# Reordering the hand-over and the close of a fused attention, soft-MoE and ELU feed-forward kernel

## The chip, the cores and the metric

The kernel runs on one core of a Trainium2 chip. The metric is the device time of one execution in microseconds; less is better. Before the change three runs took 362.8, 362.89 and 364.88 us, with a median of 362.89 us. A core has a matrix engine (TensorE, PE in the profile; its weight loads are PEld), VectorE (DVE), ScalarE (ACT), GpSimd (POOL) and SyncE (SP), which here only issues transfers. Each engine works through its own instructions strictly in order and waits on semaphores for the others. Matrix products land in PSUM, from which VectorE and ScalarE copy them to SBUF.

## What is computed

```python
for t in range(S):                                  # B=4, H=8, S=768, D=48
    state = alpha[:, :, t, :, None] * state + k_t v_t^T
    y[:, :, t] = q_t state
x = y as (3072, 384)
logits = x @ phi                                    # 32 slots
d = softmax of logits over tokens;  c = softmax of logits over slots
slot_out[e] = relu(slot_input[e] @ w1[e]) @ w2[e]   # 8 experts, slot_input = d.T @ x
x = c @ slot_out
h = x @ w_in                                        # 384 -> 2048
out = elu(h) @ w_out                                # 2048 -> 384
```

The inputs are float64 words for `w_in` and `w_out`, which the kernel converts itself, and float32 for the rest.

## The kernel before

**Stages.** Up to about 182 us the attention recurrence runs in 24 units of 128 tokens. Then come the slot softmax and, from about 202 to 231 us, the eight experts. The stage around the change follows: the expert result `o_ps` is scaled by `den` into `so`, turned (`st_ps`, `sot`) and multiplied with `w_in` into G (`g_ps`, 32 slots by 2048, laid out as four row groups of 32 by 512 columns and made in two halves x = 0, 1 of 256 columns). G is split into a rounded part `ghi` and the rest `glo`, and `g_part(x)` spreads each half into `gst` by small products (`selr`) into the banks `r_ps`, three of which are the banks `z_ps` of the last stage.

**The last stage** is a loop of 48 pairs p (6 groups of 512 tokens, 16 blocks of 128 hidden columns each, two blocks to a pair). Step 2p runs `ffn_h(p)` (two products `hf_ps`) and `ffn2(p - 2)` (six products into `z_ps`); step 2p + 1 runs `ffn_m(p)` (ScalarE makes `mm`, the ReLU of minus h, in a ring of three) and `ffn_r(p)` (r: VectorE squares the pair's first block, GpSimd its second). `hf_ps` has two buffers, so `ffn_h(p + 2)` can only start when r(p) has been read. ELU is not evaluated exactly on this path: the hidden values are small, so the kernel uses h plus half of min(h, 0) squared; the linear part is the product `gw` of G with `w_out`, added to each group's result.

**Converting w_out.** Sixteen pieces m of `w_out` are converted on the fly: `cvo_hi(m)` is two VectorE instructions (`f64_hi`, lines 85 and 87), `round_wo(m)` one of ScalarE (line 872), both needed by `ffn2(m // 2)`; `cvo_lo(m)` is one of ScalarE, one of VectorE (`f64_lo`, lines 93 and 94) and one of GpSimd (line 710), needed only by `gw_part`.

**What sets the order.** It is written out by hand. `at_place(k)` is called behind every expert and every step (place 15 + i stands behind step i) and runs whatever the tables name for that place: `HI`, `RD` and `LO` for the three conversions of each m, `GTW` for turning G, the four `gw_part` and `gw_end`, `CLOSE` for the 12 late additions, `CHK` for the checks. The late additions belong to groups 0 to 3, whose results are stored aside before gw is known: `close(i)` makes one product `cg_ps` in the single buffer `ps_f` and VectorE adds it. Groups 4 and 5 take gw as a third product in `z_ps` (line 1016).

**The end.** The checks leave one number `bad`. Behind the last step every engine loads it into a register (line 1074) and branches (line 1075) over `general_path`, a slow exact path that the inputs here never take, to the end of the program.

Of the kernel before, what the change touches and what calls it, by code (L numbers as in the profile page):

```python
# [10 lines left out]
F32 = mybir.dt.float32  # L11
# [59 lines left out]
HI = [9, 9, 9, 9, 10, 11, 12, 13, 14, 15, 16, 18, 20, 22, 24, 26]  # L71
RD = [9, 9, 11, 11, 12, 14, 15, 16, 17, 19, 20, 22, 24, 26, 28, 30]
LO = [15 + 14 + 10 * m // 3 for m in range(16)]

GTW = [35, 55, 57, 81, 83, 85]
CHK = [44, 54, 82, 94]
NLATE = 4
CLOSE = [87 + 3 * i // 2 for i in range(3 * NLATE)]
# [19 lines left out]
def general_path(tc, ctx, qka, vt, phi, w1, w2, w_in, w_out, out):  # L98
# [16 lines left out]
    for b in range(B):  # L115
        for j in range(NP):
# [36 lines left out]
    for u in range(NU):  # L153
# [4 lines left out]
        A_.copy(xt, xt_ps)  # L158
# [32 lines left out]
    for u in range(NU):  # L191
        t_ps = gp.tile([NS, 128], F32, tag="t", name="g_cps")
        T.matmul(out=t_ps, lhsT=cc[:, u, :], rhs=ident, start=True, stop=True)
        A_.copy(ct[:, 128 * u:128 * u + 128], t_ps)
# [3 lines left out]
    for d in range(ND):  # L198
# [4 lines left out]
        A_.copy(si[:, d, :], s_ps)  # L203
    so = gk.tile([128, ND, NS], F32, name="g_so")
    for e in range(NE):
# [6 lines left out]
        for f in range(8):  # L212
# [4 lines left out]
            A_.activation(ht[:, f, :], h_ps, AF.Relu)  # L217
        for d in range(ND):
# [4 lines left out]
            A_.copy(so[:, d, own], o_ps)  # L223

    def f64(src, dst):
# [6 lines left out]
        f64_lo(nc, w[:, :, 0], aa, dst, pp)  # L232
# [5 lines left out]
    for n in range(4):  # L238
# [5 lines left out]
        A_.copy(gs[:, 512 * n:512 * n + 512], acc[0][0:NS])  # L244
# [6 lines left out]
    for t in range(NG):  # L251
        cols = slice(TG * t, TG * t + TG)
        for f in range(NFT):
            h_ps = gp.tile([128, TG], F32, tag="h", name="g_fps")
            T.matmul(out=h_ps, lhsT=gs[:, 128 * f:128 * f + 128], rhs=ct[:, cols], start=True, stop=True)
            n_ = gw.tile([128, TG], F32, tag="n", name="g_n")
            V.tensor_scalar_min(n_, h_ps, 0.0)
            ex = gw.tile([128, TG], F32, tag="e", name="g_e")
# [3 lines left out]
            V.scalar_tensor_tensor(out=ex, in0=h_ps, scalar=0.0, in1=ex, op0=ALU.max, op1=ALU.add)  # L262
            for d in range(ND):
                T.matmul(out=acc[d], lhsT=wo[:, f, 128 * d:128 * d + 128], rhs=ex, start=(f == 0), stop=(f == NFT - 1))
        z = gw.tile([128, ND, TG], F32, tag="z", name="g_z")
        for d in range(ND):
            A_.copy(z[:, d, :], acc[d])
# [855 lines left out]
```

## Time and profile before

| | |
|---|---|
| Median of three runs | 362.89 us |
| Profiled execution | 366.09 us, of which its span 364.2 us |
| TensorE busy in the span | 296.0 us (81%) |
| VectorE busy | 271.6 us (75%) |
| ScalarE busy | 206.3 us (57%) |
| GpSimd busy | 176.6 us (49%) |
| Chain that ended last | VectorE 45%, TensorE 39% |
| Mean granted TensorE clock | 0.916 |

In the profile, times are microseconds from the span's start. The granted clock has two levels here: 1.00 is 2.4 GHz, 0.50 is 1.2 GHz. A float32 product is two matmul instructions, so "x6" is the six instructions of one pair's products into `z_ps` in the loop (their operands are rounded to one instruction each). Line numbers are those of the kernel before; behind line 80 the changed kernel's numbers are up to 15 higher.

### The profile page before, as it was taken

Reading aid. Unit: us, or ns where it says so; the run is one execution under the profiler, and the core shown is the slowest. Engines: PE = TensorE matmul, PEld = TensorE weight load, DVE = VectorE, ACT = ScalarE, POOL = GpSimd, SP = SyncE. Lnnn points to the kernel's source line nnn. Section 1 sums busy time; section 2 is a strip of 40 time slices with the busy share of each in tenths; the row PEclk is TensorE's granted clock in tenths of the full one; section 3 lists DMA queues with packets and bytes.
Section 4 is the critical chain, followed back from the end, with each engine's and each line's share of the span. In section 5 each row is a group of like instructions: output and inputs, shape, how many; then the busy total and the mean of one; then the engine's idle time right before and its main releaser. Section 6 shows DMA issues by size and latency. Waiting matters only on the chain.

```text
span 364.2 us, 9069 instructions
## 1 busy us (share of the span) xinstructions
PE 296.0 (81%) x3594; PEld 214.6 (59%) x3594; DVE 271.6 (75%) x542; ACT 206.3 (57%) x432; POOL 176.6 (49%) x242
## 2 busy tenths in 40 slices
PE   8666876976968786687788999868999999998991
PEld 4655755754656565565565545336877577665781
DVE  5999999999999999999952342568876546654641
ACT  1556676766857676676675222365776566533340
POOL 4364665566545564554651021013687869733340
PEclk9998798799889889888969999866999999998998
DMA  7559769795995877877179899900000000004422
GB/s 287 168 154 279 267 203 290 224 301 165 288 284 181 261 233 244 277 243 237 53 254 354 339 418 416 385 7 0 0 2 1 0 0 3 0 3 173 161 99 95
DMA packets 22354, 66.88 MB, mean 184 GB/s; under 512 B 2464, under 2 KB 8608, under 8 KB 21408
## 3 DMA queue, kind: packets, MB, share of 16 engines
q1 hardware_dynamic: 22016, 64.65, 51.7%
q10 hardware_dynamic: 288, 1.58, 1.1%
q8 instruction: 30, 0.49, 0.6%
q14 instruction: 20, 0.16, 0.1%
HBM read 61.50 MB, written 4.72 MB: 182 GB/s over the span
## 4 chain that ended last, share of the span: by engine, by line
DVE 45%; PE 39%; issue 10%; ACT 2%; DMA 2%; ACTq 0%
PE z_ps L1012 17%; DVE sfx L416 8%; DVE r L443 6%; PE hf_ps L985 6%; DVE cva L87 5%; DVE cvb L85 4%; PE h_ps L840 3%; DVE sn L521 3%; PE z_ps L862 2%; DVE wi L654 2%; DVE ring L421 2%; DVE pr L429 2%; DMA ring<-qka 2%; DVE wo L87 2%; PE g_ps L913 1%
## 5 line engine op out<-in xcount | busy, mean ns | idle before, releaser
L1012 PE MATMUL z_ps<-rr,wor 128*128 128x512 f32 x288 | 77.7, 405 | 0.8 <-DVE gst L1063 0.8
L997 POOL TENSOR_TENSOR rr<-mm 128x512 fp32r<-128x512 f32 x48 | 50.2, 1052 | 56.4 <-ACT mm L990 55.6
L990 ACT ACTIVATE mm<-hf_ps 128x1024 f32<-128x1024 f32 x48 | 48.9, 1028 | 32.4 <-PE hf_ps L985 23.3
L1012 PEld LDWEIGHTS z_ps<-rr,wor 128*128 128x128 f32 x288 | 55.5, 194 | 15.3 <-DVE gst L1063 1.6
L551 PE MATMUL y_ps<-vsr,r 128*64 128x64 f32 x768 | 42.7, 250 | 24.7 <-ACT vsr L291 24.1
L551 PEld LDWEIGHTS y_ps<-vsr,r 128*64 128x64 f32 x768 | 34.0, 158 | 34.6 <-ACT vsr L291 29.7
L996 DVE SCALAR_TENSOR_TENSOR rr<-hf_ps,mm 128x512 fp32r<-128x512 f32 x48 | 33.0, 690 | 26.7 <-ACT mm L990 26.5
L531 POOL TENSOR_TENSOR sp<-sn,sfx 128x192 f32<-128x192 f32 x44 | 23.9, 542 | 56.2 <-DVE sn L521 41.0
L479 POOL TENSOR_SCALAR_AFFINE_SELECT r<-at 64x512 f32<-64x512 f32 x48 | 39.2, 817 | 13.1 <-ACT at L472 10.2
L291 ACT COPY vsr<-sp 48x192 f32<-48x192 f32 x88 | 30.7, 349 | 17.4 <-POOL sp L531 16.2
L466 PE MATMUL at_ps<-r,ring 64*64 64x64 f32 x768 | 36.6, 244 | 4.2 <-DVE r L443 2.1
L291 ACT COPY r<-r 64x512 f32<-64x512 f32 x24 | 14.8, 615 | 38.9 <-DVE r L443 38.9
L466 PEld LDWEIGHTS at_ps<-r,ring 64*64 64x64 f32 x768 | 31.8, 155 | 7.7 <-issue 4.0
L985 PE MATMUL hf_ps<-cst,gst 128*128 128x512 f32 x96 | 32.5, 421 | 3.7 <-DVE rr L996 3.1
L651 POOL TENSOR_TENSOR wi<-wi,cvb 128x256 f32<-128x256 f32 x24 | 28.2, 1173 | 12.0 <-ACT xt L291 4.3
L416 DVE TENSOR_TENSOR_SCAN sfx<-ring,imp 128x520 f32<-128x520 f32 x24 | 30.2, 1260 | 2.3 <-DMA ring<-qka 2.3
L429 DVE TENSOR_TENSOR_SCAN pr<-ring,ini 128x520 f32<-128x520 f32 x24 | 31.1, 1295 | 0.8
L985 PEld LDWEIGHTS hf_ps<-cst,gst 128*128 128x128 f32 x96 | 17.7, 195 | 11.8 <-DVE rr L996 3.7
L443 DVE TENSOR_TENSOR r<-ring,pr 128x512 f32<-128x512 f32 x24 | 24.2, 1007 | 0.0
L710 POOL TENSOR_TENSOR wo<-wo,pp 128x384 bf16<-128x384 f32 x16 | 17.2, 1077 | 7.4 <-DVE pp L94 4.1
L454 PE MATMUL kt_ps<-ident,ring 128*128 128x128 f32 x96 | 17.8, 315 | 2.9 <-DVE ring L421 2.9
L508 PE MATMUL kv_ps<-vpr,kt 64*48 64x48 f32 x352 | 19.4, 219 | 0.0
(175 smaller groups left out, 542.5 us busy)
## 6 DMA issues: line engine op xcount, KB each, us to landing
ring<-qka SPq DMA_DIRECT2D x22, 772.5 KB, 5.4
w<-w SPq DMA_DIRECT2D x24, 512.0 KB, 5.1
w<-w SPq DMA_DIRECT2D x7, 1536.0 KB, 9.1
raw<-w_in SPq DMA_DIRECT2D x24, 256.0 KB, 2.8
wo<-w_out SPq DMA_DIRECT2D x8, 768.0 KB, 15.0
vsr<-vs SPq DMA_DIRECT2D x48, 96.0 KB, 4.9
out<-wi SPq DMA_DIRECT2D x4, 768.0 KB, 3.8
ring<-qka ACTq DMA_DIRECT2D x2, 772.5 KB, 7.6
```

The source lines that it names most:

```text
L291: (e.copy if e is A_ else e.tensor_copy)(out, in_)
L416: V.tensor_tensor_scan(out=flat(sfx)[:, ::-1], data0=a[:, 1:ACOL + 1][:, ::-1], data1=flat(imp)[:, ::-1], initial=0.0, op0=ALU.mult, op1=A ...
L429: V.tensor_tensor_scan(out=flat(pr), data0=a[:, 0:ACOL], data1=flat(ini), initial=0.0, op0=ALU.mult, op1=ALU.add)
L443: eng["q"][0].tensor_mul(split(r[:, 0]), split(qs(u)), st[u].pop("pr")[:, :, 1:])
L466: T.matmul(out=at_ps[64 - p0:128 - p0, j, t0:t0 + C], lhsT=k[p0:p0 + 64, j, t0:t0 + C], rhs=r[p0:p0 + 64, h2, j, t0:t0 + C], start=True, s ...
L479: G.affine_select(out=split(r[p0:p0 + 64, h2]), in_=split(at[p0:p0 + 64]), pattern=[[0, 2 * NP], [1, C]], compare_op=ALU.is_ge, fill=0.0, ...
L551: T.matmul(out=y_ps[t0:t0 + C, 2 * j + h2, :], lhsT=r[:, h2, j, t0:t0 + C], rhs=vsr[u % RING][:, h2, g, D * j:D * j + YW], start=True, sto ...
L985: T.matmul(out=h_ps[:, x, :], lhsT=gst[:, 128 * f:128 * f + 128], rhs=cst[:, TG * grp:TG * grp + TG], start=True, stop=True)
L990: A_.activation(m, hp[p], AF.Relu, scale=-1.0)
L996: V.scalar_tensor_tensor(out=r[0], in0=h[:, 0], scalar=-1.0, in1=m[:, 0], op0=ALU.mult, op1=ALU.mult)
L997: G.tensor_mul(r[1], m[:, 1], m[:, 1])
L1012: T.matmul(out=z_ps[j], lhsT=wo[:, cols], rhs=rs[x], start=(i == 0), stop=(late and i == NFT - 1))
```

## The change

Five things, all behind the experts. (1) `g_ps` becomes two PSUM tiles, one for each half of G; `so` is made by ScalarE alone; one small product (`busy2(1)`) stands behind `sot`, and six products into a tile `idle` behind `ffn_h(1)`. (2) The tables of conversions: of the three `cvo_hi` between the second half of G and r(0), one moves ahead of that half and one behind r(0), the `cvo_lo` are spread from place 25 to 73 (before: 29 to 79). (3) `mm` has four places instead of three. (4) The four `gw_part` stand together at place 76, `gw_end` at 77, the checks at 44, 54, 60 and 70, and the 12 late additions at 81, 83, ..., 103, one for each pair (before: two in each run of three places from 87 on). (5) In the last group ScalarE evacuates all three banks, SP stores the first and ScalarE the other two in one transfer; the register load moves up to ahead of step 92; the general path's ScalarE copies go to VectorE, so that ScalarE has about a quarter of the instructions to branch over.

```diff
-HI = [9, 9, 9, 9, 10, 11, 12, 13, 14, 15, 16, 18, 20, 22, 24, 26]
+HI = [9, 9, 9, 9, 10, 10, 11, 12, 14, 17, 18, 20, 22, 24, 26, 28]
-LO = [15 + 14 + 10 * m // 3 for m in range(16)]
+LO = [15 + 10 + 16 * m // 5 for m in range(16)]
-GTW = [35, 55, 57, 81, 83, 85]
-CHK = [44, 54, 82, 94]
+GTW = [35, 76, 76, 76, 76, 77]
+CHK = [44, 54, 60, 70]
-CLOSE = [87 + 3 * i // 2 for i in range(3 * NLATE)]
+CLOSE = [81 + 2 * i for i in range(3 * NLATE)]
...
-    A_.activation(so[:, 0:256], o_ps[:, 0:256], AF.Copy, scale=den)
-    V.tensor_scalar_mul(so[:, 256:], o_ps[:, 256:], den)
+    A_.activation(so, o_ps, AF.Copy, scale=den)
...
     A_.copy(sot, st_ps)
+    busy2(1)
...
-    g_t = ps_h.tile([128, 2, 512], F32, tag="h", name="g_ps")
-    g_ps = [g_t[:, x, 0:256] for x in range(2)]
+    g_ps = [ps_h.tile([128, 2, 512], F32, tag="h", name="g_ps")[:, 0, 0:256] for x in range(2)]
...
-        mp[p] = m = mm[:, 2 * TG * (p % 3):2 * TG * (p % 3 + 1)].rearrange("p (x t) -> p x t", x=2)
+        t, x = (mm, p % 4) if p % 4 < 3 else (end, 2)
+        mp[p] = m = t[:, 2 * TG * x:2 * TG * (x + 1)].rearrange("p (x t) -> p x t", x=2)
...
-                (A_.copy if j == 1 else V.tensor_copy)(z[:, j, :], z_ps[j])
-                if grp == NG - 1:
-                    SY.dma_start(out=out[:, j, toks], in_=z[:, j, :])
+                last = grp == NG - 1
+                (A_.copy if last or j == 1 else V.tensor_copy)(z[:, j, :], z_ps[j])
+                if last and j == 0:
+                    SY.dma_start(out=out[:, 0, toks], in_=z[:, 0, :])
+                elif last and j == ND - 1:
+                    A_.dma_start(out=out[:, 1:, toks], in_=z[:, 1:, :])
...
     for i in range(2, NK + 4):
+        if i == NK - 4:
+            b = nc.values_load(bad[0:1, 0:1], min_val=0, max_val=1,
+                               skip_runtime_bounds_check_because="a comparison gave it")
         ffn_step(i)
+        if i == 2:
+            idle = ps_f.tile([128, 128], F32, tag="f", name="idle")
+            for _ in range(6):
+                T.matmul(out=idle, lhsT=ident, rhs=ident, start=True, stop=True)
```

The diff of `general_path` (ScalarE's copies become VectorE's, two ELU blocks share an activation), of `f64_lo` (which takes the multiplying engine as an argument) and of `RD` (two entries one place earlier or later) is left out.

VectorE between the first subtraction into `glo` (line 917, now 921) and the second r: two instructions of lines 85 and 87 are one `cvo_hi`, 1063 (1071) are the copies of `g_part`, 996 (1001) is r. Before:

```order
L85 TENSOR_SCALAR pp<-wo_3178 128x384
L87 SCALAR_TENSOR_TENSOR wo_3178<-wo_3178,pp 128x384
L1063 CAST gst<-z_ps_3019 128x256
L1063 CAST gst<-z_ps_3021 128x256
L85 TENSOR_SCALAR pp<-wo_3189 128x384
L87 SCALAR_TENSOR_TENSOR wo_3189<-wo_3189,pp 128x384
L85 TENSOR_SCALAR pp<-wo_3189 128x384
L87 SCALAR_TENSOR_TENSOR wo_3189<-wo_3189,pp 128x384
L996 SCALAR_TENSOR_TENSOR rr_3440<-hf_ps,mm 128x512
```

Now, at the same place:

```order
L921 TENSOR_TENSOR gst<-g_ps,gst 128x256
L1071 CAST gst<-z_ps_3019 128x256
L1071 CAST gst<-z_ps_3021 128x256
L85 TENSOR_SCALAR pp<-wo_3189 128x384
L87 SCALAR_TENSOR_TENSOR wo_3189<-wo_3189,pp 128x384
L1001 SCALAR_TENSOR_TENSOR rr_3442<-hf_ps,mm 128x512
L1071 CAST gst<-z_ps_3019 128x256
L1071 CAST gst<-z_ps_3021 128x256
```

Between the second half's `glo` and r(0) one conversion stands instead of three, and none stands between r(0) and the second copies of `g_part`.

TensorE in the close: 974 (978) is the late addition's product, 1040 the product of the check, 985 `hf_ps`, 1012 one bank of `z_ps`. Before, at the places 93 and 94:

```order
L974 MATMUL cg_ps<-cst,gwst 128x512 x2
L1040 MATMUL n_ps<-ok_3444,ok_3443 1x1
L985 MATMUL hf_ps<-cst,gst 128x512 x2
L1012 MATMUL z_ps_3019<-rr_3440,wor_3493 128x512 x2
L1012 MATMUL z_ps_3020<-rr_3440,wor_3493 128x512 x2
```

Now, for every pair from place 81 on:

```order
L978 MATMUL cg_ps<-cst,gwst 128x512
L989 MATMUL hf_ps<-cst,gst 128x512 x2
L1017 MATMUL z_ps_3019<-rr_3442,wor_3369 128x512 x2
L1017 MATMUL z_ps_3020<-rr_3442,wor_3369 128x512 x2
L1017 MATMUL z_ps_3021<-rr_3442,wor_3369 128x512 x2
```

Two products that share the one buffer of `ps_f` no longer follow each other.

ScalarE's last rows: 990 (995) makes `mm`, 1017 (1023) evacuates a bank. Before:

```order
L990 ACTIVATE mm<-hf_ps 128x1024 x7
L1017 COPY zz<-z_ps_3020 128x512
L1074 TENSOR_LOAD bad
L1075 COMPARE_AND_BRANCH
```

Now:

```order
L1081 TENSOR_LOAD bad
L995 ACTIVATE mm<-hf_ps 128x1024
L995 ACTIVATE end<-hf_ps 128x1024
L1023 COPY zz<-z_ps_3019 128x512
L1023 COPY zz<-z_ps_3020 128x512
L1023 COPY zz<-z_ps_3021 128x512
L1027 DMA out<-zz 128x2x512
L1089 COMPARE_AND_BRANCH
```

VectorE's and SP's part of the last evacuation has moved to ScalarE, and the register load stands two pairs earlier, as on all engines.

## Rows read from the trace of the kernel before

**Rows 1.** The page: the span and the number of instructions.
```profile
span 364.2 us, 9069 instructions
```
**Rows 2.** Stretches: length, each engine's busy time, granted clock, DMA share, GB/s.
```profile
234.80:241.60 6.80, 5.46 (x52) 2.16 (x44) 1.95 (x5) 2.00 (x5) 0.00 (x0) 0.50 0.22 87
245.00:251.90 6.90, 4.48 (x10) 3.09 (x11) 6.80 (x12) 3.63 (x7) 2.59 (x3) 0.51 0.00 0
251.90:320.00 68.10, 66.87 (x313) 49.36 (x312) 43.90 (x75) 43.74 (x57) 49.55 (x48) 1.00 0.00 1
333.90:337.10 3.20, 3.20 (x9) 2.52 (x8) 0.69 (x1) 1.02 (x1) 1.04 (x1) 0.50 0.65 246
```
**Rows 3.** TensorE's waits, 230 to 252 us: total, times, longest.
```profile
PE hf_ps L985 <- DVE rr L996: 2.0, 1, 2.0
PE g_ps L913 <- ACT end L919: 1.3, 1, 1.3
PE z_ps L1012 <- DVE gst L1063: 0.8, 1, 0.8
...
PE st_ps L899 <- DVE end L894: 0.4, 1, 0.4
```
**Rows 4.** Instructions in time, 226 to 262 us: start, length, engine, what, [wait].
```profile
230.73 0.58 ACT L872 ACTIVATE wor<-wo 128x384 fp32r<-128x384 f32 x1 [2.27 <-DVE wo L87]
...
231.32 0.94 PE L791 MATMUL z_ps<-ident 128*128 128x128 f32 x6
...
244.49 1.42 DVE L87 SCALAR_TENSOR_TENSOR wo<-wo,pp 128x384 int32<-128x384 int32 x1
...
246.57 1.22 PE L985 MATMUL hf_ps<-cst,gst 128*128 128x512 f32 x2 [2.03 <-DVE rr L996]
...
248.64 2.92 PE L1012 MATMUL z_ps<-rr,wor 128*128 128x512 f32 x6 [0.85 <-DVE gst L1063]
```
**Rows 5.** The chain that ended last: start, length, what.
```profile
305.36 0.46 PE hf_ps L985 x2
305.82 1.38 PE z_ps L1012 x6
...
356.73 0.69 DVE zz L1017
```
**Rows 6.** Groups by line, VectorE, 252 to 320 us: busy, mean ns, idle before.
```profile
L996 DVE SCALAR_TENSOR_TENSOR rr<-hf_ps,mm 128x512 fp32r<-128x512 f32 x32 | 22.0, 692 | 20.3 <-ACT mm L990 20.2
...
L94 DVE TENSOR_SCALAR pp<-wo 128x384 int32<-128x384 int32 x16 | 10.9, 683 | 0.0
...
L87 DVE SCALAR_TENSOR_TENSOR wo<-wo,pp 128x384 int32<-128x384 int32 x4 | 2.2, 559 | 0.1
L85 DVE TENSOR_SCALAR pp<-wo 128x384 int32<-128x384 int32 x3 | 2.1, 694 | 0.0
```
**Rows 7.** TensorE's waits, 252 to 320 us.
```profile
PE hf_ps L985 <- DVE rr L996: 1.1, 2, 0.6
```
**Rows 8.** TensorE's waits, 320 to 358 us.
```profile
PE cg_ps L974 <- DVE wi L975: 2.3, 3, 0.8
PE n_ps L1040 <- DVE wi L975: 0.8, 1, 0.8
```
**Rows 9.** The branch over the general path: count, ns, first and last start.
```profile
L1075 SPq EVENT_SEMAPHORE  x8: 17/17/17, 362.3 to 362.8; - x8
...
L1075 ACTq COMPARE_BRANCH  x1: 50/50/50, 356.6 to 356.6; - x1
...
L1075 SPq COMPARE_BRANCH  x1: 45/45/45, 358.7 to 358.7; - x1
L1075 ACTq EVENT_SEMAPHORE  x1: 17/17/17, 359.2 to 359.2; - x1
```
**Rows 10.** The last stores: count, KB each, median us from issue to landing.
```profile
out<-zz SPq DMA_DIRECT2D x1, 768.0 KB, 3.8
out<-zz SPq DMA_DIRECT2D x3, 256.0 KB, 2.6
```

More of the change, by code (lines that the diff above doesn't have):

```diff
@@ L157, in general_path @@
         xt = gw.tile([128, ND, 128], F32, tag="xt", name="g_xt")
-        A_.copy(xt, xt_ps)
+        V.tensor_copy(xt, xt_ps)
         l_ps = gp.tile([NS, 128], F32, tag="t", name="g_lps")
@@ L167, in back @@
             T.transpose(t_ps, src[:, 128 * u:128 * u + 128], ident[0:NS, 0:NS])
-            A_.copy(dst[:, u, :], t_ps)
+            V.tensor_copy(dst[:, u, :], t_ps)
     cc = gk.tile([128, NU, NS], F32, name="g_cc")
@@ L193, in general_path @@
         T.matmul(out=t_ps, lhsT=cc[:, u, :], rhs=ident, start=True, stop=True)
[L194 removed]
+        V.tensor_copy(ct[:, 128 * u:128 * u + 128], t_ps)
     si = gk.tile([128, ND, NS], F32, name="g_si")
@@ L202, in general_path @@
                      stop=(u == NU - 1))
-        A_.copy(si[:, d, :], s_ps)
+        V.tensor_copy(si[:, d, :], s_ps)
     so = gk.tile([128, ND, NS], F32, name="g_so")
@@ L222, in general_path @@
                          stop=(f == 7))
-            A_.copy(so[:, d, own], o_ps)
+            V.tensor_copy(so[:, d, own], o_ps)
     def f64(src, dst):
@@ L252, in general_path @@
         cols = slice(TG * t, TG * t + TG)
[L253 to L258, printed above, removed]
+        for f in range(0, NFT, 2):
+            n_ = gw.tile([128, 2, TG], F32, tag="n", name="g_n")
+            ex = gw.tile([128, 2, TG], F32, tag="e", name="g_e")
+            hs = []
+            for x in range(2):
+                hs.append(gp.tile([128, TG], F32, tag="h", name="g_fps"))
+                T.matmul(out=hs[x], lhsT=gs[:, 128 * (f + x):128 * (f + x) + 128], rhs=ct[:, cols], start=True, stop=True)
+                V.tensor_scalar_min(n_[:, x, :], hs[x], 0.0)
             A_.activation(ex, n_, AF.Exp)
@@ L261, in general_path @@
             V.scalar_tensor_tensor(out=ex, in0=ex, scalar=1.0, in1=n_, op0=ALU.add, op1=ALU.mult)
-            V.scalar_tensor_tensor(out=ex, in0=h_ps, scalar=0.0, in1=ex, op0=ALU.max, op1=ALU.add)
-            for d in range(ND):
-                T.matmul(out=acc[d], lhsT=wo[:, f, 128 * d:128 * d + 128], rhs=ex, start=(f == 0), stop=(f == NFT - 1))
+            for x in range(2):
+                e = ex[:, x, :]
+                V.scalar_tensor_tensor(out=e, in0=hs[x], scalar=0.0, in1=e, op0=ALU.max, op1=ALU.add)
+                for d in range(ND):
+                    T.matmul(out=acc[d], lhsT=wo[:, f + x, 128 * d:128 * d + 128], rhs=e,
+                             start=(f + x == 0), stop=(f + x == NFT - 1))
         z = gw.tile([128, ND, TG], F32, tag="z", name="g_z")
         for d in range(ND):
-            A_.copy(z[:, d, :], acc[d])
+            V.tensor_copy(z[:, d, :], acc[d])
         SY.dma_start(out=out[:, :, cols], in_=z)
```

23 lines of the change are left out of this document (11 added, 12 removed).

## The prediction

> **What bounds the kernel now.** I read the chain that ended last first, then TensorE's waits by stage, then the stretches. Up to 231 us nothing is changed, so only what follows counts. From 251.9 to 320 us TensorE is busy for 66.87 of 68.1 us at the full clock [rows 2], and in steady state a pair is its `hf_ps` and `z_ps` products back to back, 0.46 + 1.38 = 1.84 us [rows 5]: that part is bound by TensorE and can only gain what TensorE waits there, 1.1 us in two waits [rows 7]. The time to be had lies on both sides of it. In the hand-over, TensorE waits four times for VectorE and ScalarE, 4.5 us in all [rows 3], and works at 1.2 GHz from 234.8 to 241.6 and from 245.0 to 251.9 us [rows 2]. In the close, it waits four times, 3.1 us, for a late addition to free a PSUM buffer [rows 8], and at 333.9 us, right behind these gaps, its clock falls for 3.2 us [rows 2]. After the last VectorE copy (356.73 + 0.69 = 357.4 us [rows 5]) the span runs on for 6.8 us to 364.2 [rows 1], without any compute.
>
> **Hand-over.** *Waits.* ScalarE alone makes `so`, so VectorE's queue of conversions no longer holds `st_ps`: 0.4 us. With two tiles, G's second half need not wait for ScalarE's copy out of the first half's tile: 1.3. Of the three conversions behind the second half's `glo` one is left ahead of r(0), and r(0) is what the third pair of `hf_ps` products waits for: 2.0. The second copies of `g_part` stand right behind r(0): 0.8. Sum 4.5 [rows 3].
> *Clock.* In 245.0 to 251.9 us TensorE was busy for 4.48 us at half clock [rows 2]: one pair's six `z_ps` products took 2.92 us there instead of 1.38 [rows 4, 5]. If the six idle products keep TensorE busy enough, half of 4.48 comes back: 2.2. Bounds 0 and 2.2; I take all of it, since the wait of 2.0 us right ahead of these slow products is gone too. For G the bounds are 0 and half of its 5.46 us, 2.7 [rows 2]; I take 0.4, near the low end, since ScalarE's queue is next there whatever TensorE does.
> *Costs.* The idle products are 12 instructions. Six of that shape took 0.94 us at the full clock [rows 4], so the block is at most 1.9 us, twice that at the low clock. It can only start when ScalarE has read the `r_ps` bank, but the first `z_ps` products need VectorE's copies by then anyway, so part of it covers a wait: bounds 0 and 3.8, taken 1.0. And `RD` puts two roundings instead of one ahead of ScalarE's cast of G's second half: one more of 0.58 [rows 4], taken 0.6. `busy2(1)` stands in the time in which TensorE waits for `sot`; uncovered it would cost a third of 0.94, 0.3.
> Sum: 4.5 + 2.2 + 0.4 - 1.0 - 0.6 = 5.5 us.
>
> **Loop.** Removed: the group ends fall behind the places 33, 49, 65 and 81; before, a `cvo_lo` stood at 49 and 65, now at none of the four, so one of the two waits of rows 7 should go (0.5); the other comes from turning G at place 35, which stays. Added: VectorE's queue. r, line 85 and line 87 are 0.69 + 0.69 + 0.56 = 1.94 us a pair [rows 6] against TensorE's 1.84. Before, six conversions stood behind r(0), now seven, and the first two `cvo_lo` (0.68 each [rows 6]) fall among them, at the places 25 and 28. The backlog is 7 x 0.1 + 2 x 0.68 = 2.1 us. Pair p + 2 comes 3.7 us behind pair p, and r(p) needs `hf_ps`, `mm` and itself, about 0.5 + 1.0 + 0.7; so some 1.5 us are slack: 0.6 us on the path. I take -0.5, and 0 for the loop (bounds -2.1 and +1.1). The fourth place of `mm` changes nothing while two `hf_ps` buffers keep ScalarE from running ahead. The register load at step 92 stands in queues that are ahead of the chain by then; at no row does anything wait for it.
>
> *A rule that speaks against this.* Line 87 took 1.42 us at 244.49 [rows 4], while GpSimd was at r, but 0.56 in the mean of rows 6. The Trainium skill says in "GPSIMD Engine Reference", section 1, that GpSimd's SBUF interfaces are shared with VectorE and contend with its instructions that read two SBUF inputs, which line 87 does. The long row agrees; the four short ones in the loop ran beside GpSimd for part of the time, and do not. By the rule every conversion moved behind r(0) takes its long form; that is the second rival.
>
> **Close.** One addition a pair, with a whole pair's products between two, frees the buffer in time, and the check at place 70 finds it free: 2.3 + 0.8 = 3.1 us [rows 8]. With these gaps gone the clock should stay up: half of 3.20 us, 1.6 [rows 2]. New: all four `gw_part` lie in one block; TensorE has the same products, and ScalarE and VectorE have nothing to be late with behind it. But at place 77 ScalarE's cast of gw stands ahead of pair 31's `mm`, and waits for a product behind the block; the following r is late by about one `mm` less the slack: -0.5 (bounds 0 and 1.0). Sum 4.2 us.
>
> **End.** SP stores three banks, branches at 358.7 and goes on at 362.3 us, 3.6 us later; its eight waits end at 362.8, the span 1.4 us behind them [rows 1, 9]. Now SP has only the first bank's store, which is free some 1.4 us before TensorE ends, no register load behind it, and branches about 356.4 us on the old scale: goes on at 360.0. ScalarE ends its last copy near 357.3, as VectorE did, and issues 512 KB; 256 KB land in 2.6 and 768 KB in 3.8 us [rows 10], so 3.2, at 360.6. ScalarE's own branch follows the issue, about 358; it took 2.6 us before (356.6 to 359.2 [rows 9]), now between 0 and that: 360.6 at worst. So SP's waits end near 360.9 and not at 362.8: 1.9 us (bounds 1.3, with 3.8 us to landing, and 2.4, with 2.6).
>
> **Sum.** 5.5 + 0 + 4.2 + 1.9 = 11.6 us. The profiled execution would go from 366.09 to 354.5. It lies 3.2 us above the median of the runs; I carry the difference over one to one: 362.89 - 11.6 = 351.3 us. The Trainium skill, in "TensorE: Matmul & The Clock Gate", section "Part 1: The HAM clock gate", says that the count of slow products varies from run to run of the same kernel. No run here shows that yet; by it single runs would differ by one or two microseconds either way, and the sum would stay.
>
> **Rivals.** *The clock stays low through the hand-over (0.14).* The idle products then come at half speed, as late cover that only delays: none of the 2.2, none of the 0.4, and 1 us more for the block. 11.6 - 3.6 = 8.0: 354.9 us. For it: the clock was low twice in that stretch. Against: the longest wait, 2.0 us, is gone.
> *VectorE bounds the first pairs (0.12).* Where line 87 takes 1.42 us, a pair with a conversion costs 0.69 + 0.69 + 1.42 = 2.8 us, 1.0 above TensorE's 1.84; over seven pairs, with the two early `cvo_lo`, 8.4 us less the slack of 1.5, so some 6 less than in the sum: 357 to 358 us, and up to 3.4 more where the gaps bring the clock down for another 6.9 us, 361. For it: the row of 1.42. Against: the mean of 0.56.
> *Slower (0.03).* The same queue would have to hold TensorE through all `cvo_lo` too: 11.6 + 3.6 us lost over the 29 pairs to place 73 is 0.53 us a pair. From there on it is slower than before by 1%. VectorE's mean load there is 0.69 + 0.68 / 1.6 = 1.1 us of 1.84, so line 94 would have to take three times its 0.68. At 0.6 us a pair: 368 us.
> *The split does nothing (0.04).* If G's second half waited for ScalarE's queue and not for the tile, 1.3 us are missing: 352.6. Against it: the wait ended with the copy out of the first half.
>
> **Numbers.** The forecast holds 0.62, with 348.5 to 354 as its own range; 0.05 lie below it, where G runs at the full clock. The range to 356.5 takes in the first and last rivals and a weak form of the second: 348.5 to 356.5. A measurement of this kernel can tell about 1% from no change, which is 359.3 us at the faster side. Faster by over 1%: 0.92 (all but the strong form of the second rival and the third). Within 1%: 0.05. Slower: 0.03.
>
> **What would show it.** Behind 231 us: no wait of G's second half for a copy, the third `hf_ps` without a long wait for r, the first `z_ps` products about 5 us earlier and near 1.4 us long. In the loop, waits for r of 1 us in all; several of 0.5 us before pair 10 would be the second rival. In the close, no wait of `cg_ps` and a clock of 1.00 throughout. At the end, SP going on about 3.3 us after TensorE's last product instead of 5.6. The forecast is wrong if the span from the first `z_ps` to the last grows by more than the hand-over gives.

## The result and the profile after

The changed kernel takes 352.67 us (median of four runs, 352.28 to 355.9) against 362.85 us before (362.38 to 364.88) on the same chip: ratio 0.9729, 95% interval [0.9661, 0.9797]. The forecast was 351.3 us, in a range of 348.5 to 356.5. The profiled execution took 352.37 us; the page begins with its span.

```profile
span 350.6 us, 9090 instructions
PE 293.3 (84%) x3608; PEld 216.0 (62%) x3608; DVE 269.6 (77%) x539; ACT 207.0 (59%) x434; POOL 176.3 (50%) x242
```

Against [rows 1] the span is 13.6 us shorter, more than the medians' 10.2. To see where, I cut every profile at three marks of the timeline: the first filler product behind the experts (line 791 before, 796 now), the first `z_ps` product of pair 2, and the end of the last `z_ps` product. A is the hand-over, B the rest of the loop and the close, C the end without compute.

| | marks (us) | A | B | C |
|---|---|---|---|---|
| before | 231.32, 253.91, 356.69 | 22.59 | 102.78 | 7.51 |
| changed | 230.43, 245.55, 343.78 | 15.12 | 98.23 | 6.82 |

So 0.9 us of the 13.6 lies ahead of the change (231.32 against 230.43) and is none of its doing; A gave 7.5, B 4.5 and C 0.7. In the stretches A and B (columns as in [rows 2]) the clock stayed at 2.4 GHz:

```profile
230.43:245.55 15.12, 12.97 (x117) 9.37 (x113) 13.63 (x31) 12.04 (x25) 3.81 (x4) 1.00 0.35 143
245.55:343.78 98.23, 96.49 (x437) 72.17 (x435) 63.45 (x106) 57.47 (x73) 62.96 (x61) 1.00 0.11 41
```

TensorE's waits, first from 230 to 246 us, then from 246 to 344 us:

```profile
PE hf_ps L989 <- ACT gst L1071: 1.1, 1, 1.1
PE idle L1087 <- ACT gst L1071: 0.6, 1, 0.6
PE st_ps L903 <- ACT end L898: 0.4, 1, 0.4
```

```profile
PE z_ps L1017 <- POOL rr L1002: 0.7, 1, 0.7
PE hf_ps L989 <- DVE rr L1001: 0.6, 2, 0.4
```

In the first, the four waits of [rows 3] are gone. What is left is for ScalarE, and before's list had that too, in smaller rows that [rows 3] leaves out:

```profile
PE hf_ps L985 <- ACT gst L1063: 0.4, 1, 0.4
...
PE g_ps L913 <- ACT sot L901: 0.3, 1, 0.3
PE st_ps L899 <- ACT end L893: 0.3, 1, 0.3
```

So the wait for ScalarE's part of `so` grew from 0.3 to 0.4 us, the one for `sot` went, the one for ScalarE's copy of G grew from 0.4 to 1.1, and the idle products brought one of their own, 0.6. In the second, the waits of [rows 8] are gone, and one for GpSimd is new. The first `z_ps` products start at 241.83 instead of 248.64 us:

```profile
241.83 1.56 PE L1017 MATMUL z_ps<-rr,wor 128*128 128x512 f32 x6
```

### The profile page after: what moved, and what is told of

It reads as the page before. It is cut to its first block, busy times and chain, and to the rows that moved or that the text cites. A ratio compares the mean times of both kernels' runs of the same rounds, so it can differ in the third digit from the quotient of the medians.

```text
span 350.6 us, 9090 instructions
## 1 busy us (share of the span) xinstructions
PE 293.3 (84%) x3608; PEld 216.0 (62%) x3608; DVE 269.6 (77%) x539; ACT 207.0 (59%) x434; POOL 176.3 (50%) x242
## 3 DMA queue, kind: packets, MB, share of 16 engines
q10 hardware_dynamic: 560, 2.11, 1.6%
## 4 chain that ended last, share of the span: by engine, by line
DVE 46%; PE 34%; issue 10%; ACT 5%; DMA 2%; POOL 1%; POOLq 0%; ACTq 0%
PE z_ps L1017 14%; DVE sfx L421 8%; DVE r L448 6%; DVE cva L87 5%; PE hf_ps L989 5%; DVE cvb L85 4%; PE h_ps L845 3%; DVE sn L526 3%; PE z_ps L867 3%; DVE ring L426 2%; DVE wi L659 2%; DVE rr L1001 2%; DVE pr L434 2%; DMA ring<-qka 2%; DVE wo L87 1%
## 5 line engine op out<-in xcount | busy, mean ns | idle before, releaser
L1017 PE MATMUL z_ps<-rr,wor 128*128 128x512 f32 x288 | 76.1, 396 | 0.8 <-POOL rr L1002 0.7
L556 PE MATMUL y_ps<-vsr,r 128*64 128x64 f32 x768 | 45.4, 256 | 21.1 <-ACT vsr L296 20.5
L1017 PEld LDWEIGHTS z_ps<-rr,wor 128*128 128x128 f32 x288 | 53.4, 188 | 15.3 <-POOL rr L1002 3.3
L1002 POOL TENSOR_TENSOR rr<-mm 128x512 fp32r<-128x512 f32 x36 | 38.7, 1079 | 33.3 <-ACT mm L995 32.4
L556 PEld LDWEIGHTS y_ps<-vsr,r 128*64 128x64 f32 x768 | 35.8, 161 | 31.6 <-ACT vsr L296 26.7
L995 ACT ACTIVATE mm<-hf_ps 128x1024 f32<-128x1024 f32 x36 | 36.8, 1027 | 15.6 <-PE hf_ps L989 12.5
L1001 DVE SCALAR_TENSOR_TENSOR rr<-hf_ps,mm 128x512 fp32r<-128x512 f32 x36 | 24.8, 688 | 13.2 <-ACT mm L995 13.0
L459 PE MATMUL kt_ps<-ident,ring 128*128 128x128 f32 x96 | 19.5, 338 | 2.4 <-DVE ring L426 2.4
L513 PE MATMUL kv_ps<-vpr,kt 64*48 64x48 f32 x352 | 21.1, 231 | 0.0
L513 PEld LDWEIGHTS kv_ps<-vpr,kt 64*48 64x48 f32 x352 | 17.8, 140 | 5.1 <-issue 4.7
```

The source lines that it names most:

```text
L513: T.matmul(out=kv_ps[g][p0:p0 + D, j, :], lhsT=kt[rows, j, p0:p0 + D], rhs=v, start=True, stop=True)
L556: T.matmul(out=y_ps[t0:t0 + C, 2 * j + h2, :], lhsT=r[:, h2, j, t0:t0 + C], rhs=vsr[u % RING][:, h2, g, D * j:D * j + YW], start=True, sto ...
L995: A_.activation(m, hp[p], AF.Relu, scale=-1.0)
L1002: G.tensor_mul(r[1], m[:, 1], m[:, 1])
L1017: T.matmul(out=z_ps[j], lhsT=wo[:, cols], rhs=rs[x], start=(i == 0), stop=(late and i == NFT - 1))
```

## The experiments

Each run is the changed kernel but for the edit shown (- changed kernel, + run), and gives one profile. Medians of a few runs of the same code differed by up to 2 us (352.67 and 354.65 below), so I weigh the stretches A, B and C, which repeat: B of nine runs whose loop is the changed kernel's lies between 98.23 and 98.42 us.

| run | median us | ratio, 95% | A | clock in A | B | C |
|---|---|---|---|---|---|---|
| again | 354.65 | 0.974 [0.968, 0.980] | 16.57 | 0.90 | 98.25 | 7.57 |
| old_handover | 358.08 | 0.986 [0.979, 0.994] | 20.71 | 0.84 | 97.35 | 7.01 |
| old_close | 359.59 | 0.989 [0.985, 0.993] | 15.14 | 1.00 | 102.25 | 7.27 |
| old_end | 354.88 | 0.977 [0.973, 0.982] | 16.54 | 0.90 | 98.33 | 7.72 |
| one_tile | 354.47 | 0.973 [0.969, 0.977] | 16.07 | 1.00 | 98.23 | 7.33 |
| no_idle | 352.75 | 0.968 [0.965, 0.972] | 14.83 | 0.88 | 98.42 | 7.35 |
| two_stores | 352.15 | 0.967 [0.963, 0.970] | 15.12 | 1.00 | 98.27 | 7.17 |
| sp_free | 354.07 | 0.973 [0.967, 0.979] | 15.15 | 1.00 | 98.28 | 6.86 |
| late_jump | 352.79 | 0.971 [0.964, 0.977] | 15.12 | 1.00 | 98.25 | 6.28 |
| dve_out | 353.26 | 0.973 [0.969, 0.978] | 15.11 | 1.00 | 98.27 | 6.41 |
| best | 351.41 | 0.966 [0.960, 0.971] | 15.09 | 0.89 | 97.62 | 6.64 |
| best_again | 352.97 | 0.970 [0.967, 0.973] | 16.55 | 0.79 | 97.60 | 6.92 |

**The same kernel once more.** No edit.

> The changed kernel once more, as the mark for the other kernels of this call. Expected: 352 to 353 us, with a profile like the first one, clock at 1.00 from the experts to the last product. If the length of the hand-over depends on where the clock happens to fall, this profile shows it falling behind 230 us and is 2 to 4 us longer.

The loop repeats to 0.02 us, the hand-over does not: it is 1.45 us longer, and the whole of that lies where the clock was at 1.2 GHz.

```profile
240.20:243.60 3.40, 3.20 (x14) 3.12 (x15) 3.21 (x8) 2.28 (x5) 1.60 (x2) 0.51 0.00 0
```

Ahead of it TensorE did the same work with the same waits as in the first profile of the kernel.

**The hand-over undone.**

```diff
-HI = [9, 9, 9, 9, 10, 10, 11, 12, 14, 17, 18, 20, 22, 24, 26, 28]
+HI = [9, 9, 9, 9, 10, 11, 12, 13, 14, 15, 16, 18, 20, 22, 24, 26]
...
-    g_ps = [ps_h.tile([128, 2, 512], F32, tag="h", name="g_ps")[:, 0, 0:256] for x in range(2)]
+    g_t = ps_h.tile([128, 2, 512], F32, tag="h", name="g_ps")
+    g_ps = [g_t[:, x, 0:256] for x in range(2)]
```

(`so`, `busy2(1)`, `RD` and the idle products as before the change, too; `LO` stays the changed kernel's. Of `RD` one entry moves from place 12 back to 14, one from 18 back to 19.)

> The changed kernel with the old hand-over: one tile for both halves of G, VectorE's part of so, the old tables HI and RD, no idle products; the close and the end stay new. The working of the prediction gives back 5.5 us (about 358.2). The two traces, where the first z_ps products of the second pair start 8.4 us earlier of which 0.9 us is there before anything is changed, give back 7.5 us (about 360). If a good part of the old hand-over was the clock of that one profiled execution, it is only the four waits: 4.5 less the costs of 1.6, about 355.5.

The waits of [rows 3] come back:

```profile
PE hf_ps L990 <- DVE rr L1002: 1.9, 1, 1.9
PE g_ps L918 <- ACT end L924: 1.4, 1, 1.4
PE z_ps L1018 <- DVE gst L1072: 0.7, 1, 0.7
```

and the clock falls in the longest of them, ahead of pair 2's hidden products at 243.73 us:

```profile
243.30:250.00 6.70, 5.56 (x12) 3.97 (x13) 6.00 (x11) 2.88 (x5) 2.08 (x2) 0.50 0.00 0
```

A is 20.71 us, against 15.5 in the mean of the eight profiles with the changed kernel's hand-over: it is worth 5.2. Three marks divide that. From the first filler product to G it is 3.02 us here and 2.54 to 2.58 in the eight (`so`). From G to the first hidden products it is 5.25 against 4.3 (the split). The rest, to the end of A, is 12.43 against 8.6 in their mean. Before's profile has 1.9 more; there both halves of G ran at 1.2 GHz (2.44 and 2.79 us), here at 2.4 (1.5 each), so that part is of one execution.

And B is 0.9 shorter with the old places: the new ones cost that in the loop. The rows are the changed kernel's GpSimd ahead of the wait of 0.7 us at 256.14. By the starts of the products around it this wait costs 0.9 us (256.14 - 255.02, less 0.23 for a product), which is all of the difference. r (line 1002) queues behind GpSimd's part of a `cvo_lo` (line 715), and that one waited 1.23 us for VectorE's line 94.

```profile
250.16 2.53 POOL L1002 TENSOR_TENSOR rr<-mm 128x512 fp32r<-128x512 f32 x2
253.91 1.08 POOL L715 TENSOR_TENSOR wo<-wo,pp 128x384 bf16<-128x384 f32 x1 [1.23 <-DVE pp L94]
254.91 1.19 POOL L1002 TENSOR_TENSOR rr<-end 128x512 fp32r<-128x512 f32 x1
256.05 1.07 POOL L715 TENSOR_TENSOR wo<-wo,pp 128x384 bf16<-128x384 f32 x1
```

Line 94 comes late because the new `HI` puts a conversion (lines 85 and 87) ahead of it, at place 28:

```profile
252.31 0.59 DVE L85 TENSOR_SCALAR pp<-wo 128x384 int32<-128x384 int32 x1
252.94 0.56 DVE L87 SCALAR_TENSOR_TENSOR wo<-wo,pp 128x384 int32<-128x384 int32 x1
253.41 0.35 DVE L94 TENSOR_SCALAR pp<-wo 128x384 int32<-128x384 int32 x1
```

With the old `HI` no conversion stands there. The same `cvo_lo` then waits 0.36 us, and TensorE does not wait for GpSimd at all:

```profile
259.02 1.08 POOL L715 TENSOR_TENSOR wo<-wo,pp 128x384 bf16<-128x384 f32 x1 [0.36 <-DVE pp L94]
```

**The split undone.**

```diff
-    g_ps = [ps_h.tile([128, 2, 512], F32, tag="h", name="g_ps")[:, 0, 0:256] for x in range(2)]
+    g_t = ps_h.tile([128, 2, 512], F32, tag="h", name="g_ps")
+    g_ps = [g_t[:, x, 0:256] for x in range(2)]
```

> The changed kernel with G's halves in one PSUM tile again. If the split does what the prediction said, the second half's products wait 1.3 us for ScalarE's copy out of the first half's tile, and the hand-over (experts' end to the second pair's products into the result banks) is longer by 1.3 us than the changed kernel's 13.3 to 14.7. Rival: what follows on ScalarE and VectorE, the casts and subtractions of the first half, sets the end, and the second half only comes early: then the wait is there again but the hand-over grows by 0.3 us or less.

The wait is back (1.4 us), and A is 16.07 against 15.12 at the same full clock: the split is worth 0.95 of its 1.4. The rest goes into the wait of the first hidden products for ScalarE's copy of G, which is 0.4 us here and 1.1 with the split. ScalarE's cast of G's second half (line 920) now finds two roundings ahead of it:

```profile
235.68 1.00 ACT L877 ACTIVATE wor<-wo 128x384 fp32r<-128x384 f32 x2
...
236.56 0.38 ACT L920 CAST gst<-g_ps 128x256 fp32r<-128x256 f32 x1
```

**Without the idle products.**

```diff
-        if i == 2:
-            idle = ps_f.tile([128, 128], F32, tag="f", name="idle")
-            for _ in range(6):
-                T.matmul(out=idle, lhsT=ident, rhs=ident, start=True, stop=True)
```

> The changed kernel without the six idle products behind the second pair's hidden products. As the prediction had it they cost 1.0 us and keep the clock up, worth up to 2.2: without them the first products into the result banks take 2.9 us instead of 1.56, and the stretch from the experts' end to the second pair's such products grows from 13.3 (or 14.7, where the clock fell) by about 1.2 us. Rival: the clock stays up because the long wait for r is gone, and the idle products only delay: then that stretch shrinks to 12 to 12.5 us, the first products stay at 1.4 to 1.6, and the median falls by about 1 us.

Neither theory: the clock does fall, and nothing is lost by it. The first `z_ps` products take 2.11 us instead of 1.56 but start 0.84 us sooner behind the experts (10.56 against 11.40 us). With the two profiles of the run at the end of this section the clock fell in all three without the products (A 14.83, 15.09, 16.55, mean 15.5) and in two of the eight that have them and the split (six of 15.1, 16.57, 16.54, mean 15.5). In these profiles they hold the clock more often than not and cost what that saves; eleven profiles do not tell a small gain from none.

**The close undone.**

```diff
-GTW = [35, 76, 76, 76, 76, 77]
-CHK = [44, 54, 60, 70]
+GTW = [35, 55, 57, 81, 83, 85]
+CHK = [44, 54, 82, 94]
...
-CLOSE = [81 + 2 * i for i in range(3 * NLATE)]
+CLOSE = [87 + 3 * i // 2 for i in range(3 * NLATE)]
```

> The changed kernel with the old places of the gw products, the checks and the late additions. By the working of the prediction: 3.1 us of waits and 1.6 us of low clock come back, 0.5 us of the new wait for the cast of gw goes: plus 4.2, about 356.9 us. Rival: the clock falls in the close only where the check's product follows a late addition, and its place is now different against the loop, so the clock stays: plus 2.6, about 355.3.

B is 102.25 instead of 98.23 us, 4.0 more, and the waits of [rows 8] are back to the tenth:

```profile
PE cg_ps L978 <- DVE wi L979: 2.3, 3, 0.8
PE n_ps L1048 <- DVE wi L979: 0.8, 1, 0.8
```

But the clock stays at 1.00 through this B: its fall at 333.9 us before [rows 2] does not follow from the gaps alone. The waits explain 3.1 of the 4.0. A wait row counts idle time only, and a stop costs more than that:

```profile
316.97 0.41 PE L978 MATMUL cg_ps<-cst,gwst 128*128 128x512 f32 x1
318.16 0.50 PE L978 MATMUL cg_ps<-cst,gwst 128*128 128x512 f32 x1 [0.78 <-DVE wi L979]
```

These two products start 1.19 us apart, where products in the loop start 0.23 apart [rows 5]. By the starts the four stops cost 3.9 us. `gw_part` in four separate blocks costs 0.6 more than in one, and the wait of 0.4 us that the changed kernel has for r behind gw's cast (at 308.83) is not there: by the starts 0.6 less. Together that is 3.9 of the 4.0.

**The end undone.** Stores, copies, place of the register load and the long general path of before; the cut shows the copies and stores.

```diff
-                (A_.copy if last or j == 1 else V.tensor_copy)(z[:, j, :], z_ps[j])
-                if last and j == 0:
-                    SY.dma_start(out=out[:, 0, toks], in_=z[:, 0, :])
-                elif last and j == ND - 1:
-                    A_.dma_start(out=out[:, 1:, toks], in_=z[:, 1:, :])
+                (A_.copy if j == 1 else V.tensor_copy)(z[:, j, :], z_ps[j])
+                if grp == NG - 1:
+                    SY.dma_start(out=out[:, j, toks], in_=z[:, j, :])
```

> The changed kernel with the old last evacuation and stores, the register load behind the last step and ScalarE's long general path. By the working of the prediction plus 1.9 us, about 354.6. By the two traces (6.8 us behind TensorE's last product against 7.5 before) plus 0.7, about 353.4.

C is 7.72 us, and 7.17 in the mean of the eight profiles with the new end (the two next runs, which vary it, among them): 0.55 less, or 0.3 less than before's 7.51; I take 0.4. The branch rows of the changed kernel show why it is so little:

```profile
L1089 SPq EVENT_SEMAPHORE  x8: 17/17/17, 348.7 to 349.3; - x8
...
L1089 SPq COMPARE_BRANCH  x1: 45/45/45, 343.5 to 343.5; - x1
...
L1089 ACTq COMPARE_BRANCH  x1: 54/54/54, 344.9 to 344.9; - x1
L1089 ACTq EVENT_SEMAPHORE  x1: 17/17/17, 345.4 to 345.4; - x1
```

ScalarE's jump now takes 0.5 us instead of 2.6 [rows 9], but SP goes on only at 348.7, 5.2 us behind its branch. That is the instant at which ScalarE's store, issued at 344.4, lands:

```profile
out<-zz ACTq DMA_DIRECT2D x1, 512.0 KB, 4.3
out<-zz SPq DMA_DIRECT2D x1, 256.0 KB, 2.7
```

**Does SP wait for the landing, or is its own jump slow?** Two runs: ScalarE's two banks in two stores, and SP without any last store.

```diff
-                elif last and j == ND - 1:
-                    A_.dma_start(out=out[:, 1:, toks], in_=z[:, 1:, :])
+                elif last:
+                    A_.dma_start(out=out[:, j, toks], in_=z[:, j, :])
```

> The changed kernel, but ScalarE stores banks 1 and 2 in two transfers of 256 KB instead of one of 512 KB. In the changed kernel and in three variants of it SP goes on over the branch at the instant at which ScalarE's 512 KB land, 4.3 to 4.9 us behind their issue. Theory 1: SP waits for the landing. Two transfers, the first issued one evacuation (0.8 us) earlier, both land about 2.7 us behind their issues as SP's own 256 KB do, so SP goes on some 1 to 1.8 us sooner: the tail from TensorE's last product to the span's end falls from 6.8 to 7.6 us (changed kernel, two profiles) to 5.5 to 6.3. Theory 2: SP's jump takes 5 to 6 us because its instructions are fetched beside the stores; then the landing is not what counts and the tail stays at 6.8 to 7.6. The median is expected between 353 and 354.7 us; the tail decides, not the median.

```diff
-                    SY.dma_start(out=out[:, 0, toks], in_=z[:, 0, :])
+                    A_.dma_start(out=out[:, 0, toks], in_=z[:, 0, :])
```

> The changed kernel, but ScalarE issues the store of bank 0 too, so that SP has no store behind the last step and reaches its branch several us earlier, away from the last stores. If SP's jump is long because of the fetch beside the stores (theory 2), it now takes 3.6 us or less, is over before TensorE ends, and what is left is the landing of the 512 KB: tail 6.5 or less if they land in 3.2 us, as 256 KB take 2.6 and 768 KB 3.8. If SP waits for the landing (theory 1), SP's jump ends early but its last waits still stand at the landing, 4.3 to 4.9 us behind the issue, and the tail stays at 6.8 to 7.6 us. A median within 0.7 us of the changed kernel's by theory 1, 1 to 1.5 us less by theory 2.

In the second run SP branches at 338.1 us, 6.6 us ahead of the end of TensorE's last product (changed kernel: 0.3), and that moves nothing: its waits still end at 349.7, when the 512 KB, issued at 345.5, have landed. So SP waits for the landing. In the changed kernel, too, the semaphore that SP's first wait behind the branch names has its last report at 348.72, and SP goes on at 348.74. Yet two stores do not help either: the second lands after 4.4 us, and C is 7.17. What holds the landing shows in the DMA traffic of the changed kernel, first from 345.3 to 346.7, then from 347.0 to 348.3 us (queue, packets, MB, share of 16 engines):

```profile
q10 hardware_dynamic: 235, 0.48, 89.5%
q8 instruction: 1, 0.02, 5.4%
```

```profile
DMA packets 15, 0.03 MB, mean 22 GB/s; under 512 B 1, under 2 KB 1, under 8 KB 15
...
q10 hardware_dynamic: 15, 0.03, 6.3%
```

In the second stretch 6.3% of 16 engines is one engine: fifteen have ended, and one still has packets left. In the first, one packet of 16 KB of code (queue q8) took 5.4% of 16 x 1.4 us, 1.2 us of one engine; by the packet records it begins at 345.4, 4.1 us behind TensorE's branch. In the eight profiles with the new end the last engine ends 1.2 to 2.1 us behind the other fifteen. That it is the one with the packet of code shows in four of them, where the fifteen are done before that packet ends. In the run without idle products no packet of the store moves from 347.40 to 348.44; the code takes from 347.39 to 348.46, and the last three data packets of the store follow at once. In the other three (two stores, one tile, old hand-over) the store likewise goes on within 0.02 us of the code's end.

**TensorE's branch later.** One product behind all others, which waits for ScalarE's copy out of the first bank.

```diff
+        if end_ and grp == NG - 1:
+            T.matmul(out=z_ps[0][0:1, 0:1], lhsT=ident[:, 0:1], rhs=ident[:, 0:1], start=True, stop=True)
```

> The changed kernel with one more product on TensorE, one row by one column into the first result bank, behind all others: it waits for ScalarE's last copy out of that bank, so that TensorE's queue reaches its branch about 1.8 us later (341.3 in the changed kernel, when GpSimd's last r is done; now about 343.1). In all eight profiles with the new end, 15 of 16 DMA engines have ended the last store 2.3 us behind its issue, and one drags on for 1.5 us alone, with a code fetch of 1.0 to 1.9 us ahead of its packets that begins 4.1 us behind TensorE's branch (345.4). Theory: this fetch makes the landing 4.3 to 4.9 us instead of 2.5 to 3. Shifted to about 347 it comes behind the store; the landing is then 2.5 to 3.2 us, and the end is set by TensorE's jump (3.4 us from 343.1: 346.5) or the landing near 347.3: the tail behind TensorE's last product falls from 6.8-7.6 to 5.5-6.2 us. If TensorE's first fetch (1.0 us behind its branch) now meets the store instead, the landing is 3.5 to 4 us and the tail 6.3 to 6.9. Rival: the dragging engine is slow for another reason (its share of the packets, or other engines' fetches); then the tail stays at 6.8 to 7.6 us.

TensorE branches 0.7 us ahead of the end of its last product of the loop, 1.8 us later than in the changed kernel (2.5 ahead). The first code packet of its jump, 344.9 to 346.4, now meets the start of the store, the second (348.4) comes as its last packets go, and the 512 KB land after 3.7 us; C is 6.28. With the two profiles at the end of this section the landing is 3.7, 4.0 and 4.3 us with the late branch, against 4.1 to 4.9 in seven without. That is the middle case that was expected: the code fetch is part of the landing, by some 0.6 us in the mean (4.0 against 4.6), though the two ranges overlap. Clearer is SP's own 256 KB, issued 1.4 us ahead. They now meet the first code packet and land after 3.8, 4.2 and 4.5 us with the late branch, where the profiles without it have 2.3 to 2.8; they still land before the 512 KB.

```profile
out<-zz ACTq DMA_DIRECT2D x1, 512.0 KB, 3.7
out<-zz SPq DMA_DIRECT2D x1, 256.0 KB, 3.8
```

**What ended the old end.** The rows of before that the prediction did not show are VectorE's: it goes on at 362.1, 0.2 us ahead of SP's 362.3 [rows 9].

```profile
L1075 DVEq COMPARE_BRANCH  x1: 72/72/72, 357.6 to 357.6; - x1
...
L1075 DVEq EVENT_SEMAPHORE  x1: 21/21/21, 362.1 to 362.1; - x1
```

The run is the old end with ScalarE in VectorE's place for the last copies (here - is the run with the old end):

```diff
-                (A_.copy if j == 1 else V.tensor_copy)(z[:, j, :], z_ps[j])
+                (A_.copy if grp == NG - 1 or j == 1 else V.tensor_copy)(z[:, j, :], z_ps[j])
```

> The run with the old end, with one edit: ScalarE instead of VectorE makes the copies of the last group's first and third bank; SP's three stores, the register loads behind the last step and the long general path stay. In the two profiles with the old end SP goes on over the branch 0.2 and 0.4 us behind VectorE (362.3 and 362.1; 351.2 and 350.8), and VectorE's jump, which follows its last copy, takes 4.5 us. Theory: SP waits there for VectorE, so with VectorE out of the last copies the end is set by ScalarE's jump (2.6 us, branch about 1.2 us behind TensorE's last product) or by the last store's landing (2.6 to 3 us), both some 3.8 us behind TensorE's last product: SP goes on 3.8 to 4.4 us behind it instead of 5.6 to 5.8, and the tail to the span's end is 5.7 to 6.4 instead of 7.5 to 7.7 us. The prediction's reading (SP's own jump takes 3.6 us from its branch, which does not move): tail 7.5 to 7.8, as before.

C is 6.41 instead of 7.72. VectorE is done early, and SP goes on 2.6 us behind its branch, where with the old end it took 3.6 (before) and 3.8:

```profile
L1079 SPq EVENT_SEMAPHORE  x8: 17/17/17, 348.3 to 348.9; - x8
...
L1079 DVEq EVENT_SEMAPHORE  x1: 21/21/21, 343.6 to 343.6; - x1
...
L1079 SPq COMPARE_BRANCH  x1: 45/45/45, 345.7 to 345.7; - x1
```

So VectorE's jump of 4.5 us, beside the last stores and SP's jump, cost the old end 1.1 to 1.3 us. That SP waited for VectorE, as was expected, is not what the trace shows. The eight waits behind SP's branch name semaphores of DMA queues, and the last report on any of them came at 361.64 in before, 0.6 us ahead of SP's 362.27. What SP does wait for from VectorE comes later, at 363.2 and in the closing barrier, and VectorE was ready for both by 362.2. What is longer beside VectorE's jump is SP's own: 3.6 and 3.8 us against 2.6. Why, no row shows. This one edit gives more than the change's whole new end: three stores on SP land after 2.9 to 3.1 us each, and the short general path and the early register load win nothing that shows here.

**Three edits together.** No idle products, the late product, and gw's last step behind pair 31's r.

```diff
-GTW = [35, 76, 76, 76, 76, 77]
+GTW = [35, 76, 76, 76, 76, 77, 78]
...
         V.tensor_copy(gw, gw_t[0])
+
+    def gw_last():
+        gw = end[:, DM:2 * DM]
         r_ps = ps_f.tile([128, DM], F32, tag="f", name="gwr_ps")
```

> The changed kernel with three edits: no idle products, the late product of the run before this one, and gw's last step (its product, ScalarE's cast, VectorE's two rows) one place later, behind pair 31's r instead of ahead of its mm. Expected of each against the changed kernel: idle products away, -0.3 us where the clock falls in that stretch and -1.1 where it does not (the six cost 1.1 us in the traces; in the run without them the experts' end to the second pair's result products took 12.96 us with the clock falling, against 13.3 without and 14.7 with a fall in the changed kernel); the late product, -1 if the code fetch is what holds the last store, 0 if not; gw's cast, -0.4 (the wait of pair 33's hidden products at 308.8 us). Together -0.7 to -2.5: a median of 350.5 to 353 us.

> The run with three edits once more, for its interval and a second profile. If they gain what the traces of the first show (1.3 us between the experts' end and the second pair's result products against a changed kernel whose clock fell there, 0.3 against one whose clock did not; 0.3 to 1 at the end; 0.4 at the late additions), its ratio to the kernel before is 0.965 to 0.970, below the changed kernel's two, 0.973 and 0.974. If the first result was a fast chip, it is 0.971 or above.

B is 97.62 and 97.60, 0.6 less, from the place of gw's step; C is 6.64 and 6.92, 0.4 less in the mean. A gains nothing, and in the second profile the clock was at half speed for 6.6 us:

```profile
239.80:246.40 6.60, 6.13 (x15) 4.85 (x16) 5.85 (x12) 5.47 (x10) 3.55 (x4) 0.51 0.00 0
```

The ratios, 0.966 and 0.970, lie below the changed kernel's 0.973 and 0.974, as 1.0 us of rows would have it, but the intervals overlap: the gain is shown in the rows, not yet in the time.

## Why the prediction was right, and where not

The direction, the places and most of the size held. By the experiments the change is worth 5.2 (hand-over) - 0.9 (loop) + 4.0 (close) + 0.4 (end) = 8.7 us; the two measurements of it gave 10.2 and 8.5 us, the forecast 11.6. The range held both. The second median, 354.65 us, lies above the narrower range to 354 us; that the first lies inside it is partly luck, since 8.7 us would be 354.1. Loop and end missed by 0.9 and 1.5 us, both to the slow side.

**Hand-over: 5.5 forecast, 5.2 measured, by a partly different sum.** `so` gave 0.5 for 0.4. The split gave 0.95 for 1.3 less the 0.6 of the rounding ahead of the cast, which came as that wait of 1.1 us for ScalarE's copy. From the first hidden products on it gave 3.8 for 4.0: the waits for r and for the second copies, 2.8, and the clock's 2.2 less the idle products' 1.0. The waits are gone; the *clock* is where the reasoning was off. Its 2.2 less 1.0 was taken as a gain of 1.2 by the idle products. Their cost shows as 0.84, and the clock did stay up in most profiles, but the mean gain over no idle products is nothing. *G's clock*, 0.4, cannot be told from one execution's chance: even with the old hand-over G ran at the full clock.

The first rival (clock low through the hand-over) came in one of the two profiles of the changed kernel, at 1.45 us and not the 3.6 it was priced at. What the prediction cited from the Trainium skill ("TensorE: Matmul & The Clock Gate", "Part 1: The HAM clock gate"), that the count of slow products varies from run to run of one kernel, is borne out: none slow behind the experts in one profile, 3.4 us in the other. The fourth rival fell: the split does something.

**Loop: 0 forecast, -0.9 measured** (the cost of the new `HI` and `RD`), inside the bounds of -2.1 and +1.1. The step that failed is the path of VectorE's backlog. It was weighed against VectorE's own r, with 1.5 us of slack, and taken as balanced by a removed wait. It came out through GpSimd: the conversion at place 28 holds line 94, that holds GpSimd's part of the `cvo_lo`, and behind it GpSimd's r starts 1.6 us after its `mm` (ready at 253.30, started at 254.91). GpSimd's queue was not in the sum. The removed wait was also read wrongly: the prediction put one of the two waits of [rows 7] down to turning G, but that is at 266.42, and the waits, at 282.80 and 301.24, both stand right behind a group's end. Both are gone in the changed kernel. Yet for the whole loop the two profiles leave -1.1 (B's 4.5 less the close's 4.0 and the clock's 1.6); what took back the gain of the removed waits, no run shows. The second rival (VectorE the bound) did not come: TensorE was busy for 96.49 of 98.23 us. A long form of line 87 does occur beside GpSimd:

```profile
250.52 1.27 DVE L87 SCALAR_TENSOR_TENSOR wo<-wo,pp 128x384 int32<-128x384 int32 x1
```

The rule that it was weighed against (the Trainium skill, "GPSIMD Engine Reference", section 1) agrees with this row; the next one, at 252.94 with GpSimd idle from 252.7 on, took 0.56 us. It agrees with before's rows, too, and here the prediction misread them: the four short ones of [rows 6] did not run beside GpSimd but while it was idle (one from 256.57 to 257.13, with GpSimd's r up to 256.32 and again from 257.13). The long form was too rare to decide.

**Close: 4.2 forecast, 4.0 measured, close by luck.** The waits were 3.1 us by their rows, as forecast. The clock's 1.6 was in before's profile alone: with the old close and everything else new it did not fall. Two costs that the sum lacked took its place: by the starts of the products the stops are 3.9 us and not 3.1, and the four blocks of `gw_part` cost 0.6 more than one. gw's cast ahead of pair 31's `mm` cost 0.6 where 0.5 was forecast.

**End: 1.9 forecast, 0.4 measured.** The term that was mis-sized is the landing of ScalarE's 512 KB: 3.2 us, between 2.6 and 3.8, and it took 4.1 to 4.9, outside its bounds. In the changed kernel's profile it took 4.3, and this 1.1 us is nearly all that is missing there (0.7 us for 1.9). The 2.6 us of [rows 10] is the median of three stores. Before's trace has the spread as well, and its 4.2 is the last store's, issued at 357.48 and landed at 361.64 (us from issue to landing of the three):

```profile
DMA to landing us min/median/max: 2.4/2.6/4.2
```

So the long landing of a last store could be read before the change. The other step, SP's 3.6 us as its own jump, stands, but its size does not: with VectorE's jump out of the way it is 2.6. In the changed kernel it no longer sets the end. The Trainium skill says in "Runtime: NRT & Kernel Launch", section "Instruction fetch mechanics", that a taken branch whose target is not in the pages at hand forces a fetch by DMA before the engine goes on. The trace agrees: ScalarE's jump over a quarter of the code took 0.5 us, TensorE's 3.3 to 4.4, with a packet of code in it. That such a fetch delays a store is what the run with the late branch shows, and the packets of four profiles show it on one engine.

**The carry-over to the median.** The profiled pair differ by 13.7 us, the medians by 10.2: before's profile was an execution with G and the close at 1.2 GHz, and 0.9 us late by the experts. Carrying the sum over one to one counted two of the clock's terms, 0.4 for G and 1.6 for the close, as if every execution had them; no other profile shows either. The fall that the 2.2 stands for did come again with the old hand-over.

## What to carry to other kernels

Before a price is put on what follows a program's last product, look at every landing and at every engine's jump and not at a median: of three equal stores here the last took 4.2 us and the others 2.4 and 2.6. Take what the clock costs from more than one execution, since filler products that keep it up can cost all that they save. Price a stop by the starts of the products around it, not by its idle time. And when work is moved, follow each engine's queue that it touches to the next engine that waits for it, the one with slack included.

## What was not expected of the hardware

A 512 KB store beside code fetches landed 4.1 to 4.9 us behind its issue, while 768 KB took 3.8 before [rows 10]: in the changed kernel fifteen of its DMA engines were done 2.5 us behind the issue, and the last one, with a 16 KB packet of code of 1.2 us in that time, 1.3 us later. VectorE's jump over the same code took 4.5 us when it came with the last stores (before, and the run with the old end) and 2.9 when it came ahead of them (the old end with ScalarE's copies: 340.8 to 343.6).
